# Two-head kernel on one core: half-width products in A's last stage, C transposed by TensorE

## The chip, the cores and the metric

The kernel runs on one core of one Trainium2 chip. A core has five engines that run their own instruction lists and wait for each other by semaphores: TensorE (PE, matrix products into PSUM), VectorE (DVE), ScalarE (ACT), GpSimd (POOL) and SyncE (SP). SP and POOL here mostly issue DMA transfers. The metric is the device time of one execution in microseconds; the median of several runs is compared.

## The reference, cut to what matters

Two independent parts are computed from 2048 positions and 1024 channels, and their outputs stand side by side in an output of 2048 columns.

Part A is a long convolution. k is shifted and weighted over four taps, multiplied by v, convolved with a filter of 2048 taps by FFT, and multiplied by q:

```python
kv = k_shift * v
y = irfft(rfft(kv_padded) * rfft(ssm_k_padded))[:S] + kv * ssm_D
out_a = q * y
```

Part B is a diagonal complex recurrence between two dense products:

```python
Bu = x @ B_bar.T                      # complex, 1024 states
h_t = Lam_bar * h_(t-1) + Bu_t        # for each of 2048 positions
out_b = 2 * Re(h @ C.T) + x * Dskip
```

## The kernel before, in words

All work is cut into some 1500 small tasks. The text ORDER lists them, and the kernel is built by walking through it: a word such as `a3.7.0:p7` calls the function of that name with its arguments, and the codes behind the colon give its buffers (p: one of eight PSUM banks, a: a unit of the SBUF arena, w: one of three slots for stage weights, h: one of three state slots). Each engine executes its own instructions in exactly this order; semaphores are added where one needs another's data or buffer. So the list sets every order and every buffer.

B runs in 16 blocks of 128 positions. `x` loads a block by a transposing DMA, `U` multiplies it by the transposed B (sixteen 128-column products a task), `ue` evicts. On DVE `r1` and `r2` rotate, `sc` (two scans of 1040 elements) runs the recurrence, and `r3`, `r4` rotate back; `cy` on ACT carries the state of the last block over. `y` or `yq` then multiplies by C and adds the skip term, `yq` in quarters of the array (64 rows by 64 columns), `y` with the full array. `ye` evicts, and `yst`, `ysp`, `ysh`, `ysg` store by POOL or SP, whole or in halves.

C is needed transposed in the tile CT. It has 16 blocks (8 row blocks, real and imaginary). Before, eight of them (`cx`, L439) are loaded by a transposing DMA straight into CT; the other eight are loaded plainly (`cl`, L437), transposed by eight PE transposes (`cT`, L417) and evicted by ACT (`cc`, L441). B's own matrix goes the second way (`bl`, `bT`, `bc`).

A's FFT is done in stages as matrix products. `kvm`, `kva`, `kvb`, `kvc` form kv on DVE; `am` and, for the filter, `hT` and `hm` are the first stage, whose results go through DRAM (Ys_kv, Ys_h). Sixteen pairs are read back with `lk`, `lh` and their weights with `lw` (L666). `sh`, `sk` are the second stage, `sw` or `swp` copies with real and imaginary parts exchanged, `pr` multiplies the two spectra on DVE, `sa` transforms back, `sae` evicts, `vst` stores to DRAM (Vs). The last stage reads Vs with `vl` (L736), multiplies by the constant G (`a3`, L748), evicts into an output tile (`a3e`), multiplies by q (`qm`) and stores (`ost` by POOL, `osp` by SP). `qp` loads q.

In Vs the two parities p of the row index n = 2m + p come as separate planes. Before, `a3` makes one product for each p with 128 rows and 128 columns, and the two add up in the bank: G holds zeros where an output row does not belong to p.

```python
for p in range(2):
    nc.tensor.matmul(pt, Gt[:, p, :], st["vv", n2][:, p, dh * 512:(dh + 1) * 512], start=(p == 0), stop=(p == 1))
```

Evictions from PSUM carry a "v" where DVE does them and not ACT (`a3ev` beside `a3e`).

Of the kernel before, what the change touches and what calls it, by code (L numbers as in the profile page):

```python
# [16 lines left out]
BF16 = mybir.dt.bfloat16  # L17
# [15 lines left out]
def a_constants():  # L33
    g = np.arange(NG)[:, None, None]; l = np.arange(2)[None, :, None]; cc = np.arange(2)[None, None, :]
    k1 = (2 * g + l + 0 * cc).reshape(-1); cs = (cc + 0 * g + 0 * l).reshape(-1)
    m = np.arange(128)
# [4 lines left out]
    G = np.stack([tr.T * (m % 2 == p)[None, :] * 2 / NFFT for p in range(2)], axis=1)  # L41
# [26 lines left out]
bl.5.1:a45 bT.5.1:p6 ld_par par_T:p1 bc.5.1 bl.2.0:a25 ld_F ld_w:a26 wb.0:p0 kp.0:a0 p32 wb.2:p4 wbe.0:a8 dd wb.5:p5  # L68
bl.7.0:a32 wbe.2 bl.0.1:a34 exp1 wb.4:p3 dve2 bl.5.0:a33 dve3 bT.2.0:p6 wb.6:p2 wbe.5 bl.4.0:a49 sm_pre wbe.4
bl.4.1:a17 exp2 wb.3:p7 bl.1.1:a47 bc.2.0 wb.7:p6 wbe.3 sin0 kp.1 bT.0.1:p0 bT.7.0:p4 wbe.7 wbe.6 bl.6.1:a16 bT.4.0:p1  # L70
bc.0.1 bc.7.0 bl.0.0:a46 tabA1:a24a51a14a12 kp.-1 bT.1.1:p2 x.0:a47 par_rest cl.0.0:a39 wb.1:p7 bT.5.0:p5 sin1
bl.3.0:a31 bcv.4.0 bT.0.0:p3 wbe.1 bT.4.1:p6 bc.1.1 tabA2 kring bl.3.1:a46 kvm.3:a26 gz bT.6.1:p1 bc.0.0 bl.1.0:a23
bc.4.1 U.0.2.0:a34p4 U.0.0.0:p2 sin2 bc.6.1 bl.2.1:a22 bT.3.1:p0 bc.5.0 x.1:a33 eo kvm.2:a18 kvm.1:a40 U.0.2.1
bT.1.0:p5 kva.2 cT.0.0:p1 bT.2.1:p3 bc.2.1 bT.3.0:p6 kva.1 kvb.2:a38 kva.3 bc.3.0 U.1.2.0:a36p7 stt U.1.2.1 bl.6.0:a50
bT.6.0:p3 kvb.1:a46 bl.7.1:a32 bc.3.1 U.0.1.0:p6 bT.7.1:p0 kp.-2 bc.1.0 bc.6.0 bc.7.1 U.0.1.1 U.0.0.1 ue.0.0 ue.0.1
vp.1:a48 cl.2.0:a22 z2 z1 cl.1.1:a31 cc.0.0 x.3:a21 cl.2.1:a44 ue.1.2 ue.0.2 U.0.3.0:p3 U.0.3.1 kvb.3:a32 ue.0.3
U.1.3.0:p6 U.1.0.0:p2 kvm.0:a13 cT.2.0:p0 U.1.3.1 U.1.1.0:p5 kvc.3 kvc.2 kva.0 r1.0:a48 cc.2.0 lw.1:w0 cl.1.0:a30
ue.1.3 cx.5.1 U.1.0.1 ue.1.0 cT.1.0:p3 cc.1.0 cl.3.0:a45 kvb.0:a39 am.2.1:p4p0 ae.2.1.1:a28 rta r2.0:h0 am.2.0:p6p2
cT.2.1:p1 cc.2.1 U.1.1.1 ue.1.1 cT.3.0:p3 vp.0:a42 kvc.1 U.3.2.0:a34p7 cc.3.0 ae.2.0.1 kvc.0 ae.2.0.0 kp.3 sc.0.1
U.3.2.1 hl.0.1:a24 cl.3.1:a20 cT.3.1:p0 sc.0.0 cc.3.1 am.3.0:p5p1 ae.3.1.0:a22 ae.2.1.0 r1.1:a42 hl.0.0 U.3.3.0:p3  # L80
U.3.3.1 cT.1.1:p0 cc.1.1 kp.2 hl.1.0:a48 cl.0.1:a38 ue.3.2 am.3.1:p4p1 ae.3.1.1 U.3.0.0:p6 ue.3.3 U.3.0.1 ue.3.0
ae.3.0.0 hl.1.1 am.1.1:p0p2 ae.1.1.1:a30 cx.5.0 am.0.0:p1p7 ae.0.1.0:a18 ae.3.0.1 r3.0:a12 hdv.1 ast.2 hdv.0 ast.3
U.3.1.0:p3 r4.0 ae.0.0.0 U.3.1.1 x.2:a52 cT.0.1:p5 am.1.0:p6p4 hT.0.4:p7 r2.1:h1 ae.1.0.1 am.0.1:p0p1 hT.0.7:p2
ae.1.1.0 hc.0.4:a16 hT.0.3:p4 ae.1.0.0 hT.0.0:p7 kvm.6:a12 ue.3.1 hT.0.6:p6 hc.0.3:a17 ae.0.0.1 cy.1 cc.0.1 ld_Q
hc.0.0:a46 ae.0.1.1 U.2.1.0:a44p3 r1.3:a40 U.2.1.1 ast.1 sc.1.1 U.2.2.0:p4 hc.0.7:a23 U.2.2.1 U.2.0.0:p5 ast.0 lw.0:w1
cx.6.0 cx.6.1 ue.2.2 U.2.0.1 cx.4.1 ue.2.1 hc.0.6:a20 ue.2.0 r2.3:h2 hT.0.1:p3 hT.0.2:p7 hc.0.1:a22 sc.1.0
hm.0.6.1:p1p2 hm.0.6.0:p4p6 he.0.6.0.0:a34 U.2.3.0:p0 hT.0.5:p3 hc.0.2:a41 U.2.3.1 hm.0.3.0:p5p4 he.0.6.1.1 he.0.6.1.0
he.0.3.0.0:a42 cx.7.0 kvm.5:a36 he.0.6.0.1 y.0.0.0:p7 kva.6 hc.0.5:a40 hm.0.7.1:p1p5 hm.0.3.1:p2p6 he.0.3.1.1 y.0.0.1
kvm.4:a24 he.0.3.1.0 he.0.7.1.1:a30 y.0.0.2 he.0.3.0.1 cx.4.0 cx.7.1 ue.2.3 he.0.7.1.0 y.0.0.3 hm.0.4.0:p2p6
ye.0.0:a17 hm.0.5.1:p5p4 hm.0.5.0:p0p3 he.0.4.0.0:a48 hst.0.6.1 he.0.5.0.0:a18 hst.0.6.0 he.0.5.1.0 he.0.5.0.1  # L90
y.0.1.0:p1 y.0.1.1 kvb.6:a20 he.0.5.1.1 kva.4 hm.0.4.1:p2p7 hm.0.7.0:p5p0 he.0.4.0.1 he.0.7.0.0 he.0.7.0.1 y.0.1.2
# [12 lines left out]
he.1.3.0.1 he.1.3.0.0 he.1.7.0.1 he.1.7.0.0 kva.9 y.2.0.3 ye.2.0:a19 sc.3.1 vp.4:a22 y.2.1.0:p7 hT.1.2:p2 sc.3.0
hm.1.4.1:p0p6 hm.1.4.0:p3p5 kvc.8 hT.1.5:p4 r3.3:a44 y.2.1.1 ast.7 kvb.9:a18 y.2.1.2 hst.0.7.1 hst.1.3.1 he.1.7.1.1
y.2.1.3 he.1.4.1.0:a12 he.1.4.1.1 hst.1.3.0 hc.1.5:a20 he.1.4.0.1 he.1.4.0.0 am.8.1:p5p6 r4.3 ye.2.1 hst.1.4.1
ae.8.1.1:a40 am.8.0:p0p4 U.6.1.0:a14p1 hc.1.2:a52 U.6.1.1 ae.8.1.0 x.5:a36 ae.8.0.0 hst.0.2.1 ue.6.1 r1.4:a48 ae.8.0.1
hm.1.2.0:p7p2 he.1.2.0.0:a42 kvm.11:a28 hm.1.2.1:p3p6 hst.1.4.0 yq.3.0:p0p4 vp.5:a24 he.1.2.0.1 yq.3.1 he.1.2.1.0
hm.1.1.1:p7p1 he.1.1.1.1:a46 he.1.2.1.1 yq.3.2 hm.1.5.0:p5p3 he.1.5.0.1:a34 he.1.5.0.0 x.7:a27 yq.3.3 hm.1.5.1:p3p6
hm.1.6.1:p2p1 he.1.5.1.0 U.6.3.0:p5 kvc.9 r2.4:h1 kva.11 U.6.2.0:p3 U.6.3.1 he.1.6.1.1:a12 he.1.1.1.0 kvm.10:a48  # L110
kvb.11:a52 U.6.2.1 he.1.5.1.1 yq.3.4 ue.6.3 he.1.6.1.0 cy.4 hm.1.0.0:p7p6 ue.6.2 hm.1.0.1:p5p3 yq.3.5 he.1.0.1.0:a44
he.1.0.0.0 he.1.0.0.1 he.1.0.1.1 yq.3.6 hm.1.1.0:p1p2 he.1.1.0.0 yq.3.7 ye.3.0:a26 kva.10 ysp.2 hm.1.6.0:p6p3 ast.8
U.5.3.0:a22p5 U.5.3.1 he.1.6.0.1 he.1.1.0.1 U.5.1.0:p3 am.9.0:p2p7 am.9.1:p1p0 ue.5.3 hst.1.2.1 hst.1.0.1 hst.1.0.0
he.1.6.0.0 hst.1.5.0 hst.1.7.0 ae.9.0.0:a19 ae.9.0.1 U.5.0.0:p6 sc.4.0 sc.4.1 U.5.0.1 U.6.0.0:p5 hst.1.5.1 hst.1.1.0
ld_G U.6.0.1 hst.1.6.0 hst.1.1.1 ae.9.1.0 hst.1.7.1 kvc.11 hst.1.2.0 ae.9.1.1 hst.1.6.1 U.5.2.0:p1 ue.6.0 am.11.0:p5p2
# [75 lines left out]
def full_kernel(ctx, tc, A_q, A_k, A_v, A_shift_k, A_ssm_k, A_ssm_D, B_x, B_Lre, B_Lim, B_Bre, B_Bim,  # L191
# [550 lines left out]
    E["qp"] = qp  # L742

    def a3_(n2, dh):
        pt = bank()
# [91 lines left out]
```

## Time and profile before

| | us |
|---|---|
| median of 3 runs | 350.41 (348.75 to 353.82) |
| profiled execution, whole | 348.44 |
| its span, first to last instruction | 346.5 |
| PE busy in it | 328.0 (95%) |
| DVE busy | 325.2 (94%) |
| ACT busy | 272.3 (79%) |
| POOL busy | 69.3 (20%) |

The profile is one execution recorded by the hardware. The durations of the prediction come from it, and its sum is made against 348.44, with the distance to the median added. PE's matmuls are pipelined, so their durations overlap and PE's busy share says less than the distances between starts. The granted clock of TensorE was 0.998 of full speed.

### The profile page before, as it was taken

How to read it: one execution, taken by the hardware profiler on the slowest of the kernel's cores; microseconds unless marked ns; L12 is line 12 of the kernel's file. 1: busy time of each engine (PE TensorE's matmuls, PEld its weight loads, DVE VectorE, ACT ScalarE, POOL GpSimd, SP SyncE). 2: the span in 40 equal slices, each digit the busy share in tenths (PEclk: the TensorE clock that was granted, in tenths of full speed). 3: DMA queues.
4: the chain of work that ended last, by engine and by line, in shares of the span. 5: the costliest groups of instructions: out<-in, count | busy, mean ns of one | idle time of the engine just before them, and what ended most of it. 6: DMA issues, size and time to landing. Idle time of an engine off the chain costs nothing.

```text
span 346.5 us, 11774 instructions
## 1 busy us (share of the span) xinstructions
PE 328.0 (95%) x5086; PEld 237.5 (69%) x5105; DVE 325.2 (94%) x263; ACT 272.3 (79%) x520; POOL 69.3 (20%) x114
## 2 busy tenths in 40 slices
PE   5889899999999999999999999999699999999994
PEld 2678789654856777688957877775376789754442
DVE  3999799999999999999999999999799999999991
ACT  6999999998999884599668899899689893314741
POOL 5000002142343163121100222211021133000021
PEclk9999999999999999999999999999999999999999
DMA  6999999979979879997896689999998898998995
GB/s 214 340 292 261 354 271 275 254 264 307 334 248 248 281 245 301 281 241 277 303 343 205 226 313 344 262 353 330 276 289 297 312 334 287 295 391 270 340 405 205
DMA packets 62752, 101.09 MB, mean 292 GB/s; under 512 B 29422, under 2 KB 31742, under 8 KB 62700
## 3 DMA queue, kind: packets, MB, share of 16 engines
q1 hardware_dynamic: 52652, 65.81, 63.7%
q0 software_dynamic: 10048, 34.52, 27.8%
q8 instruction: 40, 0.66, 0.8%
q14 instruction: 12, 0.10, 0.1%
HBM read 52.08 MB, written 33.55 MB: 247 GB/s over the span
## 4 chain that ended last, share of the span: by engine, by line
PE 68%; ACT 17%; DVE 7%; DMA 4%; issue 2%; SPq 1%; DVEq 0%; ACTq 0%
PE bank L468 24%; PE bank L533 15%; PE bank L515 10%; PE bank L682 4%; PE bank L720 4%; ACT BT L433 4%; PE bank L748 3%; PE bank L602 3%; DVE gslot L499 3%; PE bank L651 2%; ACT arena L608 2%; DMA wslot<-a_c_W 2%; ACT CT L441 2%; DVE arena L486 2%; ACT arena L473 2%
## 5 line engine op out<-in xcount | busy, mean ns | idle before, releaser
L468 PEld LDWEIGHTS <-BT 128*128 128x128 bf16 x2048 | 116.2, 98 | 13.0 <-issue 8.2
L468 PE MATMUL bank<-arena,BT 128*128 128x128 bf16 x2048 | 122.6, 219 | 1.6 <-DMA arena<-in_B_x_dram 0.9
L533 PE MATMUL bank<-CT,gslot 64*64 64x512 bf16 x1408 | 87.6, 377 | 0.0
L499 DVE TENSOR_TENSOR_SCAN gslot<-rtab,gslot 128x1040 bf16<-128x1040 f32 x32 | 73.0, 2312 | 0.1
L533 PEld LDWEIGHTS <-gslot 64*64 64x64 bf16 x1408 | 43.4, 107 | 23.9 <-ACT arena L698 0.6
L473 ACT CAST arena<-bank 128x512 bf16<-128x512 f32 x63 | 38.8, 655 | 11.6 <-PE bank L468 11.6
L608 ACT CAST arena<-bank 128x512 bf16<-128x512 f32 x64 | 37.2, 670 | 5.8 <-PE bank L602 4.9
L515 PE MATMUL bank<-CT,gslot 128*128 128x512 bf16 x154 | 38.1, 380 | 0.6 <-issue 0.3
L691 ACT CAST arena<-bank 128x512 bf16<-128x512 f32 x59 | 32.5, 615 | 7.8 <-PE bank L682 7.2
L486 DVE TENSOR_TENSOR arena<-arena,Z 128x4096 bf16<-128x4096 bf16 x16 | 36.5, 2284 | 2.2 <-ACT arena L473 2.1
L708 DVE TENSOR_TENSOR arena<-arena 128x4096 bf16<-128x4096 bf16 x16 | 36.3, 2285 | 1.7 <-ACT gslot L495 0.8
L728 ACT CAST arena<-bank 128x512 bf16<-128x512 f32 x61 | 33.3, 630 | 5.4 <-PE bank L720 5.3
L486 DVE TENSOR_TENSOR arena<-gslot,Z 128x4096 bf16<-128x4096 bf16 x16 | 36.6, 2288 | 0.3
L698 ACT CAST arena<-bank 128x512 bf16<-128x512 f32 x61 | 34.2, 616 | 3.3 <-PE bank L682 2.8
L659 ACT CAST arena<-bank 128x512 bf16<-128x512 f32 x64 | 35.2, 689 | 1.0 <-PE bank L651 0.7
L551 ACT CAST arena<-bank 128x512 bf16<-128x512 f32 x29 | 17.7, 616 | 16.3 <-PE bank L533 8.7
L582 DVE TENSOR_TENSOR arena<-arena 128x4096 bf16<-128x4096 bf16 (+3 forms) x16 | 30.0, 1886 | 0.1
L662 POOL DMA_DIRECT2D Ys_h<-arena x32 | 22.9, 728 | 29.0 <-ACT arena L659 23.1
L611 POOL DMA_DIRECT2D Ys_kv<-arena x16 | 10.9, 688 | 87.1 <-ACT arena L608 71.8
L515 PEld LDWEIGHTS <-gslot 128*128 128x128 bf16 x160 | 14.0, 98 | 17.1 <-issue 2.6
L702 POOL DMA_DIRECT2D arena<-arena x20 | 10.7, 538 | 70.8 <-ACT arena L691 46.9
L682 PE MATMUL bank<-arena,wslot 64*64 64x512 bf16 x256 | 21.5, 381 | 3.0 <-DMA wslot<-a_c_W 3.0
(104 smaller groups left out, 427.7 us busy)
## 6 DMA issues: line engine op xcount, KB each, us to landing
Ys_kv<-arena POOLq DMA_DIRECT2D x16, 512.0 KB, 4.9
Ys_h<-arena POOLq DMA_DIRECT2D x32, 256.0 KB, 3.8
arena<-Ys_h SPq DMA_DIRECT2D x16, 512.0 KB, 5.3
arena<-Ys_kv SPq DMA_DIRECT2D x16, 512.0 KB, 6.4
Vs<-arena POOLq DMA_DIRECT2D x16, 512.0 KB, 5.8
arena<-Vs SPq DMA_DIRECT2D x16, 512.0 KB, 6.9
arena<-arena POOLq DMA_DIRECT2D x20, 256.0 KB, 4.1
arena<-in_A_k_dram SPq DMA_DIRECT2D x8, 512.0 KB, 6.0
```

The lines of the kernel that those rows point to most:

```text
L468: nc.tensor.matmul(pu[:, w, jl, :], BT[:, 2 * jp + jl, w, d, :], xT[:, d, :], start=(d == 0), stop=(d == ND - 1))
L473: either("ue", lambda cp, i, jp: cp(st["u", i][:, :, 2 * jp:2 * jp + 2, :], st.pop(("pu", i, jp))))
L486: nc.vector.tensor_mul(m, s_, win(Z))
L499: nc.vector.tensor_tensor_scan(gf, rtab[:].rearrange("p j t -> p (j t)"), gf, 0.0, ALU.mult, ALU.add)
L515: nc.tensor.matmul(py, h[:, w, j, 2:GW], CT[:, j, w, dh * 512:(dh + 1) * 512], start=(j == 0 and w == 0), stop=False)
L533: mm = nc.tensor.matmul(st["py", i, dh][cols, cs(r)], lhs(dh, rows, c), rhs(dh, rows), start=first, stop=last)
L608: cp(st["ysb", n2][:, p, dh * 512:(dh + 1) * 512], st.pop(("pa", n2, p, dh)))
L659: cp(o, st.pop(("pb", hf, s, e, r)).rearrange("p (n c t) -> p n c t", n=2, c=2))
L682: nc.tensor.matmul(st["ps", nm, g, l][64 * dh:64 * dh + 64, :], st["w", i][rows, a * WC:a * WC + 64], st[nm, i][rows, a, dh * 512:(dh + 1) ...
L698: cp(st["x16", i][:, a, l, :], st.pop(("ps", "k", g, l)))
L708: nc.vector.tensor_mul(hab, st.pop(("x16", i)).rearrange("p a l d -> p (a l d)").unsqueeze(1).to_broadcast([P, 2, 2 * D]), hab)
L728: cp(st["vsb", i][:, a, dh * 512:(dh + 1) * 512], st.pop(("pv", g, dh)))
```

## The change

First, A's last stage. G keeps only the 64 columns that are not zero, and the product for p writes only the 64 rows of the bank that belong to p: two half-width products (128 rows by 64 columns of the array) without accumulation. Output rows then stand by parity in the tile, so q is loaded, and A's output stored, in two transfers of 64 partitions. For q each half is a word of its own (`qpa`, `qpb` by SP, `qpag`, `qpbg` by POOL).

Second, all 16 blocks of C are loaded plainly and transposed by PE: eight `cx` go, and eight each of `cl`, `cT` and `cc` come.

Third, ORDER is written anew in full: the counts of the other tasks stay, but their order, their buffers and the choice between ACT and DVE, or SP and POOL, differ throughout. Among these the fill of the table rtab moves from ACT (`rta`) to DVE (`rt`), DVE does 22 evictions instead of 23, and SP does 14 of the exchanging copies instead of 12.

```diff
-    G = np.stack([tr.T * (m % 2 == p)[None, :] * 2 / NFFT for p in range(2)], axis=1)
+    G = tr[::2].T * 2 / NFFT
...
-bc.0.0:a46 ... cl.0.0:a39 ... cx.5.1 ... cx.6.0 cx.6.1 ... cx.4.1 ... cx.7.0
+... cl.5.1:a16 ... cT.5.1:p4 cc.5.1 ... cl.4.1:a48 cl.6.1:a49 ... cT.6.1:p6
...
-    Gt = const.tile([P, 2, P], BF16, name="Gt")
+    Gt = const.tile([P, 64], BF16, name="Gt")
...
-    kr, vr, qr, oar = (a.rearrange("(m s) d -> m s d", s=16) for a in (k, v, q, out_a))
+    kr, vr = (a.rearrange("(m s) d -> m s d", s=16) for a in (k, v))
+    qr, oar = (a.rearrange("(n p s) d -> n p s d", p=2, s=16) for a in (q, out_a))
...
-    def qp(r):
-        st["qt", r] = sb(2).rearrange("p (s d) -> p s d", s=2)
-        spd(st["qt", r], qr[:, 2 * r:2 * r + 2, :])
+    def qp(dma, r, p):
+        if ("qt", r) not in st:
+            st["qt", r] = sb(2).rearrange("p (s d) -> p s d", s=2)
+        dma(st["qt", r][64 * p:64 * p + 64, :, :], qr[:, p, 2 * r:2 * r + 2, :])
...
-            nc.tensor.matmul(pt, Gt[:, p, :], st["vv", n2][:, p, dh * 512:(dh + 1) * 512], start=(p == 0), stop=(p == 1))
+            nc.tensor.matmul(pt[64 * p:64 * p + 64, :], Gt[:], st["vv", n2][:, p, dh * 512:(dh + 1) * 512], start=True, stop=True)
...
-    E["osp"] = lambda r: spd(oar[:, 2 * r:2 * r + 2, :], st["ot", r])
+    def ostore(dma, r):
+        for p in range(2):
+            dma(oar[:, p, 2 * r:2 * r + 2, :], st["ot", r][64 * p:64 * p + 64, :, :])
+    E["ost"] = lambda r: ostore(gpd, r)
+    E["osp"] = lambda r: ostore(spd, r)
```

Three places of the order matter for what follows. The first is ACT in the opening stretch, just after block 0 has been evicted for the first rotation (COPY into CT is `cc`, CAST is an eviction of `ue` or `am`). Before:

```order
L441 COPY CT<-bank_97 128x8x128
L473 CAST arena<-bank_103 128x2x256
L473 CAST arena<-bank_100 128x2x256
L473 CAST arena<-bank_99 128x2x256
L441 COPY CT<-bank_96 128x8x128
L473 CAST arena<-bank_102 128x2x256
L473 CAST arena<-bank_98 128x2x256
L441 COPY CT<-bank_99 128x8x128
L608 CAST arena<-bank_96 128x512
L379 COPY rtab<-r 128x8x128
```

And now (lines have shifted by three):

```order
L476 CAST arena<-bank_103 128x2x256
L611 CAST arena<-bank_102 128x512
L444 COPY CT<-bank_100 128x8x128
L476 CAST arena<-bank_96 128x2x256
L362 ACTIVATE Z_77<-Z_77 128x1024
L444 COPY CT<-bank_102 128x8x128
L444 COPY CT<-bank_100 128x8x128
L611 CAST arena<-bank_97 128x512
L476 CAST arena<-bank_103 128x2x256
```

The fill of rtab has left ACT, the copies into CT go on longer (16 in all instead of 8), and evictions of kv's first stage stand among them earlier.

The second place is PE where the first products of A's last stage stand. Before, behind a quarter-array yq of block 13:

```order
L533 LDWEIGHTS gslot_89
L533 MATMUL bank_97<-CT,gslot_89 64x512
L748 LDWEIGHTS Gt
L748 MATMUL bank_101<-arena,Gt 128x512
L748 LDWEIGHTS Gt
L748 MATMUL bank_101<-arena,Gt 128x512
```

And now, behind the last U of block 15 and ahead of a yq of block 12:

```order
L471 LDWEIGHTS BT
L471 MATMUL bank_97<-arena,BT 128x128
L755 LDWEIGHTS Gt
L755 MATMUL bank_100<-arena,Gt 64x512
L755 LDWEIGHTS Gt
L755 MATMUL bank_100<-arena,Gt 64x512
```

The two products of a bank are half as wide, and the first of them stand nearer to the last product of the stage ahead: `sa` and first `a3` were 12 U tasks and 8 yq tasks apart and are now 11 and 4.

The third place is POOL near the end (L731, now L734, stores to Vs; L702, now L705, is the exchanging copy; L745 a half of q; L558, now L561, a store of B's output). Before:

```order
L702 DMA arena<-arena 64x2048
L731 DMA Vs<-arena 128x2x1024 x5
L558 DMA out_dram<-arena 128x1024
L731 DMA Vs<-arena 128x2x1024 x2
L558 DMA out_dram<-arena 128x1024
```

And now:

```order
L745 DMA arena<-in_A_q_dram 64x2048
L705 DMA arena<-arena 64x2048
L745 DMA arena<-in_A_q_dram 64x2048 x3
L734 DMA Vs<-arena 128x2x1024 x4
L745 DMA arena<-in_A_q_dram 64x2048 x2
```

Three halves of q now stand on POOL just ahead of the last four stores to Vs, which every read of the last stage waits for.

More of the change, by code (lines that the diff above doesn't have):

```diff
@@ new lines @@
+skev.30.0 pr.15 vst.9 sa.21:p0p7 vst.11 sae.21.0:a36 sae.21.1 yq.11.3 ysp.10 lw.12:w0 sh.25:p1p2 sh.24:p6p3
+she.25.0:a18 shev.24.1 sa.20:p0p7 she.25.1 yq.11.4 vst.7 she.24.0 r1.12:a8 sk.24:p1p2 skev.24.1:a28 sae.20.0
+sk.25:p3p6 ske.25.1 qpa.5:a48 lk.14:a14 yq.11.5 ske.24.0 ske.25.0 lw.14:w2 r2.12:h0 sa.31:p6p0 sae.31.0:a22 yq.11.6
+lh.13:a16 swp.12.1 sae.20.1 sae.31.1 sw.12.0 cy.12 sh.29:p1p2 shev.29.1:a40 she.29.0 sa.30:p3p6 saev.30.1 yq.11.7
+lw.13:w1 yev.11.1:a12 sh.28:p7p0 she.28.1 ye.11.0 shev.28.0 vst.10 sk.29:p1p2 ske.29.0:a0 U.13.1.0:a4p6 U.13.1.1
@@ L188 @@
+qm.2 osp.3 yev.15.0:a52 osp.7 y.15.1.1 ysh.15.0 y.15.1.2 osp.2 y.15.1.3 ye.15.1 ysh.15.1
 """
@@ L737, in full_kernel @@
     E["vl"] = vl
-    def qp(r):
-        st["qt", r] = sb(2).rearrange("p (s d) -> p s d", s=2)
-        spd(st["qt", r], qr[:, 2 * r:2 * r + 2, :])
-    E["qp"] = qp
+    def qp(dma, r, p):
+        if ("qt", r) not in st:
+            st["qt", r] = sb(2).rearrange("p (s d) -> p s d", s=2)
+        dma(st["qt", r][64 * p:64 * p + 64, :, :], qr[:, p, 2 * r:2 * r + 2, :])
+    for p_, e_ in enumerate("ab"):
+        for q_, dma_ in (("", spd), ("g", gpd)):
+            E["qp" + e_ + q_] = lambda r, p=p_, dma=dma_: qp(dma, r, p)
     def a3_(n2, dh):
```

239 lines of the change are left out of this document (117 added, 122 removed).

## The prediction

> **What bounds the kernel now.** I read the stages first, then the idle rows inside them, then the tail. Columns of the stages: us of the span, its length, then busy us of PE, PE's weight loads, DVE, ACT and POOL with instruction counts, the granted clock, the DMA share and GB/s.
>
> ```profile
> 0.00:40.00 40.00, 31.17 (x404) 25.50 (x405) 32.08 (x63) 36.57 (x60) 5.01 (x16) 1.00 1.01 293
> 40.00:160.00 120.00, 118.86 (x1658) 87.07 (x1673) 120.00 (x94) 106.44 (x201) 35.86 (x52) 1.00 0.93 277
> 160.00:230.00 70.00, 69.28 (x1357) 54.25 (x1355) 68.86 (x37) 58.43 (x119) 10.62 (x18) 1.00 0.86 285
> 230.00:254.00 24.00, 20.91 (x419) 13.67 (x416) 20.67 (x13) 19.68 (x40) 3.11 (x6) 1.00 1.00 306
> 254.00:290.00 36.00, 36.00 (x655) 27.46 (x648) 34.80 (x24) 31.27 (x63) 9.42 (x15) 1.00 0.94 303
> 290.00:316.00 26.00, 25.89 (x485) 17.62 (x485) 25.47 (x17) 5.90 (x12) 0.72 (x1) 1.00 0.93 333
> 316.00:342.20 26.20, 25.91 (x130) 11.97 (x130) 23.36 (x21) 13.47 (x28) 4.03 (x7) 1.00 0.95 335
> 342.20:346.50 4.30, 0.00 (x0) 0.00 (x0) 0.00 (x0) 0.53 (x1) 0.53 (x1) 0.82 0.31 108
> ```
>
> VectorE (DVE) never rests from 40 to 160 us and hardly after that. Up to 316 us it idles 7.9 + 0 + 1.1 + 3.3 + 1.2 + 0.5 = 14.0 us; its last link to the output, the rotation r4 of block 15, ends soon after. TensorE (PE) looks as full, but its busy time counts overlapping matmuls. So I add up PE's list by start-to-start distances, read off rows such as these:
>
> ```profile
> 42.02 1.95 PE L468 MATMUL bank<-arena,BT 128*128 128x128 bf16 x32
> 187.79 0.45 PE L682 MATMUL bank<-arena,wslot 64*64 64x512 bf16 x4
> 188.01 0.88 PE L533 MATMUL bank<-CT,gslot 64*64 64x512 bf16 x12
> 320.01 2.75 PE L748 MATMUL bank<-arena,Gt 128*128 128x512 bf16 x12
> 340.11 1.03 PE L515 MATMUL bank<-CT,gslot 128*128 128x512 bf16 x4
> 341.03 1.03 PE L515 MATMUL bank<-CT,gslot 128*128 128x512 bf16 x4
> ```
>
> A 128-column matmul or transpose takes (1.95 - 0.22)/31 = 0.056 us. A full 512-column matmul takes (2.75 - 0.38)/11 = 0.216. Four quarter-array matmuls together take 188.01 - 187.79 = 0.22, as long as one full one. A y part takes 341.03 - 340.11 = 0.92, all eight of a block 7.4. With these, PE's list is 313 us of work against its end at 342.1, so PE has some 29 us of gaps, and DVE is the tighter list. Both meet in the tail:
>
> ```profile
> 315.00 0.68 DVE L755 CAST arena<-bank 128x512 bf16<-128x512 f32 x1
> 315.60 1.21 DVE L505 TENSOR_TENSOR gslot<-arena 128x2048 bf16<-128x2048 bf16 x1
> 329.29 3.49 DVE L757 TENSOR_TENSOR arena<-arena 128x2048 bf16<-128x2048 bf16 x3
> 332.69 1.22 DVE L505 TENSOR_TENSOR gslot<-arena 128x2048 bf16<-128x2048 bf16 x1
> 341.89 0.22 PE L518 MATMUL bank<-Dd,arena 128*128 128x128 bf16 x1
> ```
>
> r4 of block 15 ends at 332.69 + 1.22 = 333.9 us. The y parts of block 15 need 7.4, which is 341.3; PE ends at 342.1. **PE's backlog in the tail is worth only 0.8 us unless DVE comes earlier too**; then come 4.4 us of eviction and store to 346.5.
>
> **The change part by part.** *Last stage of A.* 64 full matmuls of 0.216 us, 13.8 us, become 32 pairs. The trace shows no half-width pair, so its cost is bounded by two rows: four quarters together take 0.22, and two full ones one after the other 0.43. A pair's cost lies between, so the saving is between 0 and 6.9 us. I take 6.9, since the quarters too stream two operands through the same rows and write both halves of one bank. Against it stand changes of array shape:
>
> ```profile
> 305.43 0.39 PE L533 MATMUL bank<-CT,gslot 64*64 64x512 bf16 x4
> 305.75 1.47 PE L748 MATMUL bank<-arena,Gt 128*128 128x512 bf16 x5
> ```
>
> 305.75 - 305.43 = 0.32 us instead of 0.22, so 0.10 a change. In PE's order of the whole program the shape changes 64 times before and 74 times now, 13 of them behind the first yq of block 12 instead of 3: 1.0 us. [...]
>
> *C by transposes on PE.* Eight blocks more, each eight transposes on PE and one eviction on ScalarE (ACT):
>
> ```profile
> 41.07 1.24 ACT L379 COPY rtab<-r 128x1024 f32<-128x1024 f32 x1
> 42.02 1.20 ACT L441 COPY CT<-bank 128x1024 bf16<-128x1024 bf16 x1
> 42.92 0.79 ACT L473 CAST arena<-bank 128x512 bf16<-128x512 f32 x1
> 319.03 1.56 ACT L755 CAST arena<-bank 128x512 bf16<-128x512 f32 x3
> ```
>
> PE gets 64 x 0.056 = 3.6 us. ACT gets 8 x (42.92 - 42.02 = 0.90) = 7.2 us in the stretch where it has nearly no idle time. The rtab fill, 42.02 - 41.07 = 0.95 us, goes from ACT to DVE. There the trace doesn't show it; a DVE cast half its size takes 0.60 from start to start and r4's longer tensor op 1.22, so 0.6 to 1.2, and I take 1.2. Counted up to the carry copy of block 2 (cy.2), ACT's list holds eight CT copies and one BT copy (also about 0.9) more, and the rtab fill and four 0.49 us casts net fewer ((1.56 - 0.58)/2 = 0.49): 80 us become 85. DVE's list before the scans of block 2 grows from 77 to 81. So ACT runs ahead or behind by what it did: the largest lead of ACT's sum over DVE's, over all blocks, is 4.8 us before (block 0) and 4.5 after (block 1). DVE's early idle time stays. PE waits for ACT to free banks: for each product I set ACT's sum up to the cast that frees its bank against PE's sum up to the product. The largest lead goes from 14.1 us (a transpose of the filter, hT) to 15.5 (a filter product, hm), so I add 1.4 to PE's path. On the other side eight DMA transposes go:
>
> ```profile
> CT<-in_B_C_im_dram SPq DMA_TRANSPOSE x4, 5.7
> CT<-in_B_C_re_dram SPq DMA_TRANSPOSE x4, 5.6
> arena<-in_B_C_re_dram SPq DMA_DIRECT2D x4, 256.0 KB, 5.8
> wslot<-a_c_W SPq DMA_DIRECT2D x16, 160.0 KB, 4.0
> arena<-Vs SPq DMA_DIRECT2D x16, 512.0 KB, 6.9
> ```
>
> Transposes and plain loads land equally fast, and no engine waited for CT. I cost the transfers at 0; the cover is ACT's backlog, and if loads came late the y parts of block 0 would wait, at most one landing of 5.8 us. The gain has the same bound: at most one landing of 5.7, if transposes held the SP queue.
>
> *q and output halves.* The bytes are unchanged; there are 8 more loads and 8 more stores. q is off the path, since most of it is loaded before the Vs reads. An issue takes 0.3 to 0.7 us on queues that are not full; I take 0, with at most the last store's 0.4 on the path. On the POOL queue, though, three q halves now stand just ahead of the last four Vs stores, at the 0.72 us that an issue takes there (row below), 2.2 in all; the last stores wait for their casts anyway, so this is counted in the readback.
>
> *The order.* Everything moves. DVE's list up to r4 of block 15 loses seven casts of 0.60 (four a3, two y, one BT), and one q product of (3.49 - 1.22)/2 = 1.14; it gains six casts, the rtab fill of 1.2 and 0.16 for a skip add: 0.4 us less. DVE's path is then 333.9 - 0.4 + 7.4 = 340.9 plus or minus its idle time. The one long stall in the middle is a weight load:
>
> ```profile
> 243.68 0.34 SPq L666 DMA_DIRECT2D wslot<-a_c_W  x1
> 251.07 0.63 PE L682 MATMUL bank<-arena,wslot 64*64 64x512 bf16 x8 [3.01 <-DMA wslot<-a_c_W]
> 251.59 0.69 DVE L691 CAST arena<-bank 128x512 bf16<-128x512 f32 x1 [2.31 <-PE bank L682]
> ```
>
> Three slots hold the weights of 16 pairs. A load waits for the last sa of the pair that held its slot; until the new pair's first product PE had 4.4 us of work at this place, and the load took 7.3. In the new order that distance is 4.0 for the same pair 10, and 3.8, 3.8 and 3.5 for pairs 9, 11 and 14 (4.9, 5.1, 4.8 before). The usual 4.0 us landing still fits barely; a 7 us one doesn't. So the 3.0 us can go (a load that lands in 4 us) or come back two or three times, +6. I take half of it gone, -1.5.
>
> Last, the readback of Vs, which gates the a3 products:
>
> ```profile
> 290.17 0.72 POOL L731 DMA_DIRECT2D Vs<-arena  x1 [1.90 <-ACT arena L728]
> 294.77 3.90 SPq L736 DMA_DIRECT2D arena<-Vs  x6
> ```
>
> From the last store's issue to the first load's is 4.6 us, and the load lands 6.9 later; with the casts ahead some 14.6 us from the last sa. Between the last sa and the first a3 PE had 18 us of other work and has 13.4 now. The difference, 14.6 - 13.4 = 1.2, is what PE would wait; up to 2.2 more if the q issues hold the stores, 0 if PE arrives late. I add 1.0 (0 to 3.4).
>
> **The sum**, on PE's path: 342.1 - 6.9 + 1.0 + 3.6 + 1.4 - 1.5 + 1.0 = 340.7, which DVE's 340.9 less half of its 3.3 us stall allows. With 4.4 of tail the span is 345.1. The profiled execution took 348.44 for a span of 346.5, 1.94 more: 347.0. It lay 1.97 below the median of the runs, 350.41, so on that scale I say **349.0**. Below 2%, 7 us, no measurement of this kernel tells it from no change.
>
> **Rivals.** *The weight slots bind.* For: the shorter distances above, and DMA shares of 0.93 to 1.00 in those stages. Against: most loads land in 4.0, and PE has gaps there. It is slower than before from the point where two loads take 7 us: each costs PE, and DVE behind it, 7.3 - 3.8 = 3.5; three of them instead of the taken -1.5 give 349.0 + 1.5 + 10.5 = 361.0, two 357.5. Chance 0.17.
>
> *The pairs run one after the other.* No row shows them together. PE keeps its 6.9: 355.9. Against it: the four quarters. Chance 0.08. [...]
>
> *The order closes DVE's gaps.* Of the 14.0 us idle, 6.1 lie behind 40 us. If the new order avoids all of it, r4 ends at 333.9 - 0.4 - 6.1 = 327.4, and 7.4 + 4.4 + 1.94 + 1.97 make 343.1; PE's shorter a3 allows it only if PE's gaps shrink with it. Chance 0.22.
>
> *The easing of DMA does nothing and ACT's copies reach DVE.* If all 7.2 - 0.95 = 6.3 us arrive in DVE's chain: 355.3. Against it the equal leads. Chance 0.08.
>
> **How the numbers follow.** The forecast has 0.45. Its unknowns (one slot stall more or less, the readback, the drain) span 345 to 353. With the rivals at 343 and 356 in the range, 342 to 357.5 leaves the worst of the slots and an order better than bounded out, some 2 in 10. Faster by 2% (below 343.4) is most of the third rival, 0.18; slower by 2% (above 357.4) most of the first, 0.13; the rest 0.69.
>
> **What would show it.** Right: starts of two L755 matmuls of one bank a few ns apart and pairs 0.22 apart; ACT without idle to about 90 us; r4 of block 15 ending near 332; PE's idle before the first Gt product 0 to 2 us. Wrong: pairs 0.43 apart, several waits for wslot of 3 us, DVE idle beyond 8 us in the first 50 us, or waits of a3 for Vs over 3 us.
>
> The likeliest error is in the sum of small idles, since both lists end within a microsecond of each other and any stall on either shows in full.

## The result and the profile after

| | before | changed |
|---|---|---|
| median of the runs | 349.58 us (347.16 to 353.82) | 357.88 us (357.04 to 365.15) |
| ratio to before, 95% interval | | 1.027 (1.021 to 1.032) |
| profiled execution, whole / span | 348.44 / 346.5 | 357.04 / 355.3 |
| DVE busy in it | 325.2 | 325.4 |

The changed kernel is 2.7% slower; the forecast was 349.0. (Here and below the ratios leave disturbed executions out, while a median takes all; a ratio is the safer of the two.) The 8.8 us between the spans are not work: DVE is busy as long as before. So they are waits, and the first question is in which stage they arose. These are the windows of the changed kernel, with the columns of the prediction's first fence:

```profile
0.00:40.00 40.00, 29.84 (x365) 25.67 (x367) 32.60 (x67) 36.08 (x59) 4.98 (x15) 0.96 0.99 310
40.00:160.00 120.00, 118.36 (x1670) 87.41 (x1681) 117.73 (x92) 107.33 (x194) 33.69 (x48) 1.00 0.79 250
160.00:230.00 70.00, 69.95 (x1338) 52.19 (x1337) 68.86 (x38) 58.95 (x119) 13.55 (x23) 1.00 0.98 305
230.00:254.00 24.00, 23.70 (x475) 15.32 (x476) 23.67 (x16) 20.41 (x42) 4.38 (x7) 1.00 0.96 335
254.00:290.00 36.00, 34.34 (x620) 24.75 (x612) 32.97 (x23) 29.70 (x61) 9.59 (x16) 1.00 0.97 303
290.00:316.00 26.00, 20.64 (x342) 17.01 (x338) 20.11 (x13) 8.74 (x20) 3.83 (x6) 0.93 0.97 244
```

DVE's idle time up to 290 us is 7.40 + 2.27 + 1.14 + 0.33 + 3.03 = 14.2 us, against 13.6 before. From 290 to 316 it is 5.89 against 0.53, and PE has lost about as much (20.64 us busy instead of 25.89). In the same stretch the DMA engines are as busy as before (0.97 against 0.93) but move 244 GB/s instead of 333. The stall can be followed in the rows of PE, ACT and DVE, taken from their timelines, and in the chain of waits:

```profile
301.39 7.00 PE L471 MATMUL bank<-arena,BT 128*128 128x128 bf16 x96 [4.21 <-DMA arena<-in_B_x_dram]
307.53 1.56 ACT L476 CAST arena<-bank 128x512 bf16<-128x512 f32 x3 [9.45 <-PE bank L471]
308.15 2.29 DVE L489 TENSOR_TENSOR arena<-arena,Z 128x4096 bf16<-128x4096 bf16 x1 [4.86 <-ACT arena L476]
```

```profile
285.31 16.04 DMA arena<-in_B_x_dram
301.39 6.12 PE bank L471 x80
307.53 0.59 ACT arena L476
308.15 2.30 DVE arena L489
```

The transposing load of x for block 15 was issued at 285.31 us and landed 16.0 us later; the median of the sixteen is 6.4. U of block 15 waits for it. The last product of block 14 stands behind these products in PE's order, so it waits too; its eviction by ACT ends at 308.1, and DVE has waited for that with `r1`, the first rotation, of block 14. What else was under way is seen in the issues between 264 and 300 us (count, size of one, median time to landing):

```profile
Vs<-arena POOLq DMA_DIRECT2D x7, 512.0 KB, 10.7
arena<-in_A_q_dram POOLq DMA_DIRECT2D x7, 256.0 KB, 10.5
arena<-in_A_q_dram SPq DMA_DIRECT2D x6, 256.0 KB, 11.6
```

Thirteen of the sixteen q halves are issued here, and much of what lands among them is late: the stores to Vs take 10.7 us in the median, where all sixteen before took 5.8. (Not all of it: the three weight loads here land in 3.5.) That delays the readback too. On POOL's queue the last store to Vs, on SP's the first read:

```profile
297.26 0.73 POOL L734 DMA_DIRECT2D Vs<-arena  x1 [3.71 <-ACT arena L731]
308.04 1.90 SPq L739 DMA_DIRECT2D arena<-Vs  x3
```

They are 10.8 us apart, where before it was 4.6. Last, the end of the program:

```profile
339.25 1.22 DVE L508 TENSOR_TENSOR gslot<-arena 128x2048 bf16<-128x2048 bf16 x1
348.97 1.46 SPq L767 DMA_DIRECT2D out_dram<-arena  x2
349.17 0.59 ACT L554 CAST arena<-bank 128x512 bf16<-128x512 f32 x1 [6.43 <-issue]
350.52 0.73 SPq L558 DMA_DIRECT2D out_dram<-arena  x1
```

r4 of block 15 ends at 340.5 instead of 333.9 us: 6.6 us. PE ends at 349.1, 8.6 behind it where it was 8.2 before: 0.4. From there to the end it takes 6.2 instead of 4.4: 1.8. The last eviction was ready at 349.76, but SP was still issuing two halves of A's output, so the last store went out at 350.52 and took 0.73 us to issue instead of 0.34. The three add up to the 8.8.

### The profile page after: what moved, and what is told of

The parts are those of the page before. It is cut to its first block, busy times and chain, and to the rows that moved or that the text cites. A ratio compares the mean times of both kernels' runs of the same rounds, so it can differ in the third digit from the quotient of the medians.

```text
span 355.3 us, 11935 instructions
## 1 busy us (share of the span) xinstructions
PE 329.6 (93%) x5151; PEld 238.2 (67%) x5169; DVE 325.4 (92%) x265; ACT 280.2 (79%) x526; POOL 73.0 (21%) x119
## 4 chain that ended last, share of the span: by engine, by line
PE 69%; DMA 12%; ACT 10%; DVE 4%; issue 3%; SPq 1%; DVEq 0%
PE bank L471 23%; PE bank L536 18%; PE bank L518 8%; DMA arena<-in_B_x_dram 5%; DMA arena<-Vs 3%; PE bank L685 3%; PE bank L605 3%; PE bank L723 3%; ACT BT L436 3%; PE bank L629 2%; PE bank L654 2%; PE bank L420 2%; DMA arena<-arena 2%; DVE arena L489 2%; PE bank L755 1%
## 5 line engine op out<-in xcount | busy, mean ns | idle before, releaser
L471 PEld LDWEIGHTS <-BT 128*128 128x128 bf16 x2048 | 118.2, 99 | 19.0 <-issue 10.2
L471 PE MATMUL bank<-arena,BT 128*128 128x128 bf16 x2048 | 125.2, 220 | 5.5 <-DMA arena<-in_B_x_dram 4.2
L536 PE MATMUL bank<-CT,gslot 64*64 64x512 bf16 x1408 | 88.9, 378 | 0.4 <-ACT arena L694 0.2
L536 PEld LDWEIGHTS <-gslot 64*64 64x64 bf16 x1408 | 41.3, 107 | 28.1 <-ACT arena L694 1.2
L476 ACT CAST arena<-bank 128x512 bf16<-128x512 f32 x63 | 40.5, 660 | 22.1 <-PE bank L471 21.7
L611 ACT CAST arena<-bank 128x512 bf16<-128x512 f32 x62 | 36.7, 654 | 5.5 <-PE bank L605 5.1
L694 ACT CAST arena<-bank 128x512 bf16<-128x512 f32 x58 | 32.1, 611 | 7.8 <-PE bank L685 7.7
L662 ACT CAST arena<-bank 128x512 bf16<-128x512 f32 x64 | 37.2, 725 | 1.4 <-PE bank L654 1.3
L701 ACT CAST arena<-bank 128x512 bf16<-128x512 f32 x59 | 33.7, 617 | 4.7 <-PE bank L685 2.9
L731 ACT CAST arena<-bank 128x512 bf16<-128x512 f32 x60 | 33.3, 613 | 4.9 <-PE bank L723 4.6
L554 ACT CAST arena<-bank 128x512 bf16<-128x512 f32 x30 | 18.4, 630 | 14.9 <-issue 9.1
L420 PE MATMUL bank<-ident,arena 128*128 128x128 bf16 x256 | 21.0, 249 | 9.3 <-DMA arena<-in_B_B_im_dram 4.2
L420 PEld LDWEIGHTS <-arena 128*128 128x128 bf16 x256 | 19.1, 113 | 11.4 <-DMA arena<-in_B_B_im_dram 5.7
```

The source lines that it names most:

```text
L420: nc.tensor.transpose(pt[:, d, :], src[:, d * P:(d + 1) * P], ident[:])
L471: nc.tensor.matmul(pu[:, w, jl, :], BT[:, 2 * jp + jl, w, d, :], xT[:, d, :], start=(d == 0), stop=(d == ND - 1))
L476: either("ue", lambda cp, i, jp: cp(st["u", i][:, :, 2 * jp:2 * jp + 2, :], st.pop(("pu", i, jp))))
L536: mm = nc.tensor.matmul(st["py", i, dh][cols, cs(r)], lhs(dh, rows, c), rhs(dh, rows), start=first, stop=last)
L611: cp(st["ysb", n2][:, p, dh * 512:(dh + 1) * 512], st.pop(("pa", n2, p, dh)))
L662: cp(o, st.pop(("pb", hf, s, e, r)).rearrange("p (n c t) -> p n c t", n=2, c=2))
```

## The experiments

Two suspicions came from these rows. **Shape**: a transfer to 64 partitions keeps the DMA engines busy longer than its bytes say. **Place**: the new order puts too many transfers ahead of the ones that matter, whatever their shape.

**The shape alone, in the changed kernel.**

```diff
-        dma(st["qt", r][64 * p:64 * p + 64, :, :], qr[:, p, 2 * r:2 * r + 2, :])
+        dma(st["qt", r][:, p, :], qw[:, 2 * r + p, :])      # qw: q as "(m s) d -> m s d"
```

> The changed kernel, with each half load of q (64 partitions x 4 KB) replaced by a load of 256 KB over all 128 partitions (2 KB each), at the same place, on the same queue, in the same number. The rows of q then stand in the old layout, so A's output multiplies the wrong rows of q; nothing else is left out. Theory 1 (a transfer to 64 partitions keeps the DMA engines busy up to twice as long, and the 13 halves between 264 and 299 us hold up what is queued behind them): the transpose of x for block 15 lands in under 9 us instead of 16.0, the DMA engines move over 300 GB/s between 290 and 316 us instead of 244, r4 of block 15 ends at 334 to 337 us instead of 340.5, time 350 to 354. Theory 2 (the new order alone: so many loads stand ahead of the transpose and of the Vs reads, whatever their shape): landing 14 to 16 us, r4 at 339 to 341, time 356 to 359.

Measured 358.2 us, ratio 1.024 (1.016 to 1.032): nothing gained, and the transpose still took 14.8 us. Taken by itself this speaks for place. It turned out to be half of the answer.

**The transpose issued earlier.**

```diff
-... sae.29.1:a0 x.15:a38 qpb.6 ...
+... lw.13:w1 x.15:a38 yev.11.1:a12 ...
```

> The changed kernel with one transfer moved: the DMA transpose of x for block 15 is issued right behind the last weight load (pair 13), ahead of eight of the q halves instead of behind them. If its late landing alone makes the loss (PE waits 4.2 us at 301.4, DVE 4.9 at 308.2): r4 of block 15 ends at 334 to 336 us, time 350 to 352. If the whole stretch is slow because the DMA engines are held by the q halves (theory 1) or by too many transfers (theory 2): the transpose comes in time, but the last Vs store still lands near 308 us and the a3 products wait for the Vs reads, so PE ends 2 to 4 us earlier at most, time 353.5 to 356.

Measured 357.6 us, ratio 1.013 (0.998 to 1.028), too wide to tell it from either kernel. The profile tells more. In the profiled execution no transpose is late (8.4 us at most), but DVE stalls 7.3 us elsewhere (its timeline):

```profile
294.22 2.29 DVE L710 TENSOR_TENSOR arena<-arena 128x4096 bf16<-128x4096 bf16 x1 [7.31 <-DMA arena<-in_A_q_dram]
```

L710 is `pr`, the product of two spectra, which doesn't read q. It needs an exchanging copy from POOL's queue, and what released it is a half of q on that queue, issued at 282.50 us and landed 11.6 us later. The copies that POOL issued between 279 and 290 us took 12.6 us in the median. So in this execution the late transpose was not the cause but the first thing to be hit; mended alone, the loss moved to the next. It took 359.2 us, though, and the shortest of the four 352.1, so it isn't shown that the loss moves so in every execution.

**The last-stage part undone in the changed kernel's order.**

```diff
-            nc.tensor.matmul(pt[64 * p:64 * p + 64, :], Gt[:], ..., start=True, stop=True)
+            nc.tensor.matmul(pt, Gt[:, p, :], ..., start=(p == 0), stop=(p == 1))
...
-        dma(st["qt", r][64 * p:64 * p + 64, :, :], qr[:, p, 2 * r:2 * r + 2, :])
+        dma(st["qt", r], qr[:, 2 * r:2 * r + 2, :])         # once, where the first half stood
```

> The changed kernel with the last-stage part undone and the rest kept: a3 as two full 128x128 products with zero columns, q and A's output as whole 512 KB transfers over 128 partitions (each whole q load stands where its first half stood, on that half's queue; so the bytes of q come slightly earlier). Theory 1: the transpose of block 15 lands in under 9 us, r4 of block 15 ends at 334 to 337; PE has its 6.9 us of a3 products back, of which some 2 to 4 show behind r4, time 351 to 356. Theory 2: landing of 14 us or more, r4 near 340, and the 6.9 us on top: 358 to 364.

Measured 356.6 us, ratio 1.018 (1.008 to 1.027). The transpose took 13.1 us, but here nothing waits long for it: PE 0.9 us, and DVE goes into `r1` of block 14 without a wait. DVE stalls on exchanging copies instead, 4.3 us in two waits. Whole loads at this place don't bring the old time back, but PE has its full products again as well, so the run doesn't say how much of the 1.8% is the loads.

**The last-stage part alone, in the order of before.** The changed kernel's functions are built from the old ORDER, `qp` issuing both halves on SP.

> The kernel before, in its own order and with C by transposes of the DMA as before; only the last stage of A is changed (pairs of half-width products; each q load becomes two half loads back to back on the SP queue, each output store two half stores on the queue it was on). By the terms of the prediction (pairs save 6.9 us of PE, of which DVE's chain lets 0.8 show; halves cost nothing): 349 to 351, ratio 0.995 to 1.00. Theory 1: five of the eight q loads stand between 290 and 330 us among the Vs reads; each takes the engines some 1.3 us longer than before, Vs reads land 2 to 4 us later, time 352 to 356.

Measured 359.5 us, ratio 1.021 (1.009 to 1.033). This part alone, without C and without the new order, costs what the whole change costs.

**No q, and q late.** Next the transfers of q were taken out of the stretch, by leaving them away and by issuing them later.

```diff
-... qpb.0:a44 sae.24.0 r3.12:a28 qpag.2:a46 qpag.4 qpbg.5 ... vl.7:a28 ... vl.14:a22 ...
+... qs.0:a44 sae.24.0 r3.12:a28 qs.2:a46 ... vl.7:a28 qpa.0 qpb.0 ... vl.14:a22 qpa.4 qpb.4 ...
```

`qs` only takes the buffer. In e_noq the late issues are missing as well, and the tile of block 1 stands in for the others.

> The changed kernel without seven of the eight q loads (14 half loads, 3.5 MB; only block 1 of q is loaded, and A's output is multiplied by it everywhere, so the loads of the other blocks of q are left out). All instructions of the engines stay. Theory 2 (so many bytes of q stand ahead of the transpose for block 15, the last swaps and the Vs stores and reads; at some 300 GB/s the 2.9 MB between 264 and 288 us are 10 us of transfers): with them gone the transpose lands in under 9 us, DVE's idle time before r1 of block 15 falls from 19.2 to 13 or 14 us, r4 of block 15 ends at 333 to 336, time 349 to 352. Theory 3 (the loss is not in the transfers of q at all but in the order of the other work): idle time of DVE stays at 17 us or more, time 356 or more.

> The changed kernel with the same 14 half loads issued later: each tile keeps its place in the arena from where it was, but the two halves are issued on the SP queue among and behind the last Vs reads, as five of the eight whole loads of q stood before. Nothing is left out. Theory 2: DVE's idle time before r1 of block 15 falls to 13 or 14 us; the Vs reads behind the first late halves land 1 to 3 us later and the products of q wait up to 3 us; time 350 to 354. Theory 3: no change, 356 to 359.

> The changed kernel once more, on the chip of these runs, so that the other three can be held against it and not only against the kernel before. Expected 356 to 359, and in its profile the same late transpose of block 15 (14 to 16 us to its landing) if that belongs to the order of issue and not to one execution; 6 to 9 us if it was chance.

The changed kernel again: 358.2 us, 1.023 (1.015 to 1.032), with a transpose that took 15.7 us, so this belongs to the kernel and not to one execution. Without q: 352.0 us, **1.008** (1.004 to 1.013). The q transfers therefore make 5 to 6 of the 8 us. Issued late they cost more still: 366.8 us, 1.049 (1.042 to 1.057), which neither theory had expected. The reason is in the window from 316 to 342 us:

```profile
316.00:342.00 26.00, 16.23 (x172) 7.26 (x166) 17.03 (x11) 10.46 (x22) 1.23 (x2) 0.86 1.05 205
```

The DMA engines are busy all the time (a share of 1.05) and move 205 GB/s. That brought the shape back in.

**The shape at the other two places, and the halves without the pairs.** e_before_ports and e_qlate_ports are e_before_pairs and e_qlate with the edit of e_ports; e_before_halves is e_before_pairs with full products.

```diff
+    G = np.zeros((128, 2, 128))
+    for p in range(2):
+        G[:, p, 64 * p:64 * p + 64] = tr[::2].T * 2 / NFFT
```

> e_qlate with the same replacement (loads of q over 128 partitions x 2 KB, wrong rows of q). e_qlate moved 205 GB/s between 316 and 342 us with the DMA engines busy all the time, where the kernel before moved 335. Theory 1: the rate comes back to 300 or more and the time to 351 to 356. Theory 2: the rate stays below 260 GB/s, time 362 to 368.

> e_before_pairs with each half load of q (64 partitions x 4 KB) replaced by a load of the same bytes over 128 partitions (2 KB each), so that A's output multiplies the wrong rows of q. Theory 1 (64 partitions take the DMA engines twice as long): back to 349 to 352. Theory 2 (number and place of the transfers): 356 to 361 as e_before_pairs.

> The kernel before, in its own order, with q and A's output in half transfers as in the changed kernel, but with a3 as two full 128x128 products (the constant's zero columns arranged so that the rows come out in the halves' order). Held against e_before_pairs it leaves the half-width pairs out and nothing else. If the half transfers alone made e_before_pairs 2% slower: 356 to 361, and the pairs are worth 0 to 2 us there. If the pairs (their changes of array shape, PE waiting otherwise) made it: 350 to 352.

e_qlate_ports took 357.1 us, 1.016 (1.010 to 1.023), some 10 less than e_qlate. Bytes, queue, place and number of transfers are the same; only 128 partitions are written instead of 64, with 2 KB each instead of 4. Its row for the same window, and the q landings of e_qlate and of e_qlate_ports:

```profile
316.00:342.00 26.00, 21.88 (x223) 10.55 (x224) 22.14 (x18) 15.43 (x32) 3.01 (x5) 1.00 1.03 366
```

```profile
arena<-in_A_q_dram SPq DMA_DIRECT2D x14, 256.0 KB, 13.9
```

```profile
arena<-in_A_q_dram SPq DMA_DIRECT2D x14, 256.0 KB, 8.5
```

366 GB/s instead of 205. What PE waited for reads of Vs between 250 and 350 us in e_qlate (us in all, times, longest) shows the price:

```profile
PE bank L758 <- DMA arena<-Vs: 15.0, 3, 6.0
```

In e_qlate_ports it is 3.1 us. (The profiled execution of e_qlate was its longest, 369.9 us; the others took 363.9 to 368.8.) (205 and 366 GB/s stand as 0.56 to 1, but reads of Vs to all 128 partitions are among them, so this is no measure of one transfer.) In the old order e_before_ports came to 351.9 us, 1.001 (0.996 to 1.006), against 1.021 for e_before_pairs and 1.013 (1.002 to 1.024, median 360.2) for e_before_halves. So **the half-partition loads of q are the loss there, and the pairs are neither its cause nor a gain**; the half stores of A's output, which e_before_ports keeps, cost nothing that shows either. PE's waits for Vs behind 290 us go the same way: 5.3 us in e_before_pairs, none in e_before_ports. One reservation: in the profiled executions of e_before_pairs and of e_before_halves part of the delay stands ahead of the first q load. POOL issues the same two exchanging copies before and in e_before_pairs at

```profile
219.77 1.06 POOL L702 DMA_DIRECT2D arena<-arena  x2 [5.25 <-PE bank L682]
```

```profile
224.00 1.06 POOL L702 DMA_DIRECT2D arena<-arena  x2 [8.63 <-ACT arena L691]
```

and the first half load follows at 235.8. In e_before_ports these copies go out at 218.94, so a part of its advantage in the profiles is not q's. What made these 4 us was not found; the size of the effect in this order rests on the comparison of the runs, not on that profile.

**Queue and shape together.** Why then did the shape not matter in the changed kernel's own order? Nine of the sixteen halves stand on POOL's queue there.

```diff
-... qpag.2:a46 qpag.4 qpbg.5 ... qpbg.7 ... qpbg.2 ...
+... qpa.2:a46 qpa.4 qpb.5 ... qpb.7 ... qpb.2 ...
```

> The changed kernel with all 16 half loads of q issued on the SP queue, at the same places of the program (nine of them stood on POOL's). If POOL's queue is the matter (half loads issued there ahead of Vs stores and swaps hold these back): the Vs stores land in under 7 us again, 351 to 355. If it is the bytes in that stretch or the shape: 355 to 360.

> e_sp with the half loads over 128 partitions x 2 KB (A's output multiplies the wrong rows of q). If the shape costs on the SP queue alone, as e_before_ports and e_qlate_ports have it, and e_ports hid that because most halves stood on POOL's queue: 351 to 354, at least 4 us below e_sp. If the bytes ahead of the last swaps, stores and the transpose make the loss: within 2 us of e_sp and of e_ports, 355 to 360.

e_sp: 356.5 us, 1.024 (1.019 to 1.029). e_sp_ports: **352.3 us, 1.013** (1.007 to 1.018). Neither edit alone helps, both together win back most of what leaving q out won. Their windows from 290 to 316 and from 316 to 342 us show how (e_sp, then e_sp_ports):

```profile
290.00:316.00 26.00, 23.24 (x435) 17.67 (x436) 25.24 (x15) 9.80 (x22) 2.76 (x4) 1.00 0.92 283
316.00:342.00 26.00, 21.74 (x236) 10.03 (x231) 19.29 (x15) 16.83 (x34) 1.90 (x4) 1.00 1.04 304
```

```profile
290.00:316.00 26.00, 24.48 (x453) 18.30 (x449) 25.57 (x15) 11.20 (x23) 2.76 (x4) 1.00 0.92 299
316.00:342.00 26.00, 25.40 (x246) 12.25 (x248) 23.20 (x18) 15.84 (x32) 3.00 (x5) 1.00 0.99 344
```

With all halves on SP, DVE's stall in the first window is gone (25.24 us busy instead of 20.11) and the longest transpose takes 8.0 us. But then DVE is busy only 19.29 us of the second: reads of Vs land late and PE waits for them. With 128 partitions as well, both shrink (landing, then PE's wait behind 300 us; e_sp, then e_sp_ports):

```profile
arena<-Vs SPq DMA_DIRECT2D x16, 512.0 KB, 12.2
PE bank L755 <- DMA arena<-Vs: 5.8, 5, 1.8
```

```profile
arena<-Vs SPq DMA_DIRECT2D x16, 512.0 KB, 9.2
PE bank L756 <- DMA arena<-Vs: 1.9, 2, 1.1
```

So two losses stand one behind the other. With halves on POOL's queue the stores on it land late (between 264 and 300 us in 10.7 us in the changed kernel and in 10.4 in e_ports, in 7.6 in e_sp), and the stall of block 15 comes with that; with halves of 64 partitions, on SP, the reads of Vs land in 12.2 us in e_sp, against 9.2 over 128 in e_sp_ports. Whichever is taken away, the other sets the end. Two things stay open. Why loads on POOL's queue also delay a transpose on SP's is not shown. And the move to SP changes times as well as the queue: the two halves that POOL issued at 298 us go out at 312.9 and 322.3, so 11 stand between 264 and 300 us instead of 13, and in e_sp DVE waits 1.9 us for one of them as data. How much of the gain is the queue and how much the later issue was not separated.

**The C part.** It was undone in the changed kernel, and with the last-stage part undone and q issued late.

```diff
-... cl.5.1:a16 ... cT.5.1:p4 cc.5.1 ...
+... cx.5.1 ...                                             # blocks 4 to 7, real and imaginary
```

> The changed kernel with the C part undone: blocks 4 to 7 of C, real and imaginary, come by DMA transposes again, each issued where its plain load stood; the 64 transposes on PE and eight copies on ACT go. If C costs what the prediction took for it (3.6 us of PE's list, 7.2 of ACT's, of which 3.6 + 1.4 on the path): 351 to 354. If these lie in slack, since the loss stands behind 290 us: within 1.5 us of the changed kernel, 356 to 359.

> The changed kernel with the last-stage part undone (a3 full, q and A's output whole, as e_whole) and q issued late as in e_qlate, so that only C and the order of the rest differ from the kernel before. If q's transfers are the loss: 350 to 354 (the 1.9 us of DVE's idle time that e_noq still had, and PE's full products). If the rest of the order costs more than that: 355 to 360.

> e_whole_qlate with the C part undone as well (blocks 4 to 7 by DMA transposes where their plain loads stood; 64 transposes on PE and eight copies on ACT less). What is left of the change is the order alone. If C costs the 1% that e_whole_qlate had over the kernel before: 349 to 351.5. If the order does, and C is hidden: 352 to 355. If the eight DMA transposes among the other loads of the first 80 us cost more than the copies did: above 355.

e_cx scattered from 356.1 to 365.8 us, median 364.8, and gives no interval; it doesn't come out faster than the changed kernel. e_whole_qlate took 353.5 us, 1.011 (1.006 to 1.015), and e_wq_cx 359.0 us, 1.029 (1.022 to 1.036). In this order the plain loads are the better way by 5 to 6 us, the opposite of the 5 us that the prediction charged for them. Their windows from 40 to 160 and 230 to 264 us (e_whole_qlate, then e_wq_cx):

```profile
40.00:160.00 120.00, 118.10 (x1660) 87.12 (x1674) 116.93 (x93) 107.33 (x193) 32.57 (x47) 1.00 0.79 250
...
230.00:264.00 34.00, 33.40 (x630) 21.58 (x629) 32.46 (x22) 28.60 (x59) 5.90 (x9) 1.00 0.97 342
```

```profile
40.00:160.00 120.00, 114.68 (x1570) 83.58 (x1584) 116.04 (x93) 99.61 (x182) 32.51 (x46) 0.99 0.87 255
...
230.00:264.00 34.00, 31.84 (x587) 20.07 (x586) 30.69 (x21) 25.99 (x53) 5.16 (x8) 0.95 0.90 311
```

ACT and PE have less to do, as foreseen, and DVE is held up all the same, 0.9 us in the first window and 1.8 in the second. With the transposes the DMA engines are busier in the first window (0.87 against 0.79), and SP is held longer: in the chain that ended last in e_wq_cx, two of them take 4.9 and 5.4 us to issue from 44.4 us on, where a plain load of C takes 0.33 at that place, and the load of x behind them goes out at 54.8 us instead of 51.6. But no single wait carries the loss, and most of them stand earlier here than they did before; it can't be said what C alone would be worth in the old order.

No version tried beats the kernel before. e_noq, e_sp_ports and e_whole_qlate, three ways to remove the cost of q, end within 1.008 to 1.013 of it; that last 1%, order and tail, was not taken apart.

## Why the prediction was wrong, by its own steps

**q and output halves at 0: this step failed.** It reasoned that the bytes are the same, that an issue takes 0.3 to 0.7 us, and that q is off the path since most of it is loaded early. The bytes are the same; the time of the engines is not: the queue that carries SP's transfers moves 65.81 MB both in e_before_pairs and in e_before_ports, but its packets take 66.2% of 359.1 us of all engines in the one and 64.4% of 350.9 in the other, so 237.7 against 226.0. q was off the path as data, but seven of its halves were issued by POOL among the seven stores to Vs between 264 and 300 us, in a stretch with a DMA share of 1.02. Leaving the loads out won 5 to 6 us (e_noq), and all of them on SP over 128 partitions about 4 (e_sp_ports). The three halves ahead of the last Vs stores were seen, but priced as issue time, 2.2 us, and not as transfers: the stores among the halves landed in 10.7 us, against 5.8 before. Where 0.4 us was allowed for the last store, the end behind PE grew by 1.8.

**The last stage of A: right.** Rows of PE's timeline in the changed kernel:

```profile
311.71 0.39 PE L536 MATMUL bank<-CT,gslot 64*64 64x512 bf16 x4
312.03 2.85 PE L471 MATMUL bank<-arena,BT 128*128 128x128 bf16 x48
314.89 0.84 PE L755 MATMUL bank<-arena,Gt 128*64 128x512 bf16 x6
320.83 0.39 PE L536 MATMUL bank<-CT,gslot 64*64 64x512 bf16 x4
321.15 1.05 PE L755 MATMUL bank<-arena,Gt 128*64 128x512 bf16 x8
```

Three pairs take 0.84 us and four 1.05, so (1.05 - 0.38)/3 = 0.22 a pair, as taken; the rival that they run one after the other falls. A change of shape costs 312.03 - 311.71 - 0.22 = 0.10 us, and from quarters to halves the same (321.15 - 320.83 - 0.22). The 1.0 us that the sum adds for ten such changes, and that the forecast calls the drain, rested on the step from quarters to full products alone. No run shows the 1.0 us as a whole; the changed kernel shows the 0.10 of one change at half-width products too. That PE's backlog is worth little unless DVE comes earlier was also right: e_before_ports, which has the pairs, is no faster than before.

**C: a term with the wrong sign.** The 3.6 us of PE and 1.4 of ACT's lead were put on the path. In the first 40 us DVE idles 7.40 us against 7.92, and 2.27 in the next 120 against none, so at most 2 us show. Against it stands what the transposing loads cost, taken as 0: e_wq_cx, which has them, is 5 to 6 us slower than e_whole_qlate in this order. The prediction had named the condition, transposes that hold the SP queue, and the bound, 5.7, but gave it no weight. The fill of rtab took 0.67 us, near the lower end of its range:

```profile
38.66 0.67 DVE L382 COPY rtab<-r 128x1024 f32<-128x1024 f32 x1
```

**The weight slots: right direction, and the rival fell.** The 3.01 us wait is gone. The only one left on PE is

```profile
280.59 0.84 PE L685 MATMUL bank<-arena,wslot 64*64 64x512 bf16 x12 [0.51 <-DMA wslot<-a_c_W]
```

so 2.5 us of the wait were won where 1.5 were taken. The shorter distances, from which the slow case was built, did no harm.

**The readback of Vs: the wait was real, its size and place were not.** From the last store to the first read it became 10.8 us, with 1.0 (at most 3.4) put on the path. In the changed kernel it hides behind the stall of block 15, and PE's own waits for Vs come to 0.2 us; in e_sp, where that stall is gone, PE waits 5.8 us for Vs.

**The rival that the order closes DVE's gaps** did not come: up to 290 us the idle time is 14.2 us against 13.6. The rival on ACT's copies did not either. Of the signs of being wrong only one showed, and weakly: DVE idles 8.9 us in the first 50 us, where 8 was the mark and 7.9 the value before. A wait of 2.2 us for ACT in it is there in e_wq_cx too, without the eight further copies. The case that came, transfers off the path that delay those on it, was not among the rivals and had no sign. The measured 357.9 lies 0.4 us above the range, whose upper end had been set for the slots.

## What to carry to other kernels

Cost a transfer by its shape and its queue, not by its bytes alone: here loads of 64 partitions cost some 10 us more than the same bytes over 128 (e_qlate, 366.8 us, against e_qlate_ports, 357.1), and loads that hardly anything waits for as data cost 5 to 6 (the changed kernel, 358.2, against e_noq, 352.0). Where the DMA engines are busy nearly all the time (0.97 here), list what is in flight beside each transfer on the critical chain before an edit of transfers is called free. And when one late transfer is found, mend it alone before blaming it: if the loss moves to the next wait, look for what the two share.

## What the runs showed of the hardware that was not expected

- With loads of 64 partitions by 4 KB among reads of Vs, the DMA engines moved 205 GB/s at a share of 1.05 (e_qlate, 316 to 342 us); with the same bytes as 128 partitions by 2 KB, 366 GB/s at 1.00 (e_qlate_ports). The halves landed in 13.9 and 8.5 us.
- While nine of the halves were issued by POOL, their shape made no measurable difference (ratios 1.024 over 128 partitions, 1.023 and 1.027 over 64); with all on SP it made about 1.1% (1.013 and 1.024).
- A transposing load took 16.0 us to land among half loads on both queues (15.7 in a second execution); among loads over 128 partitions it took 14.8, and among whole ones 13.1. It took 8.0 at most when all halves were on SP, and 7.0 at most without them.
- A transposing load of C took 1.2 to 2.6 us of SP to issue before, where the plain ones took 0.35 to 0.58; in e_wq_cx it took up to 5.4, where a plain one at that place took 0.33.
